# Two interleaved attention and gated-MLP layers on one core: operands, places and buffers in layer one's first gate/up pass

## The chip, the cores and the metric

The kernel runs on one core of one Trainium2 chip. The metric is device time in microseconds (us) of one execution; lower is better. The engines of a core are named as the profile names them: PE (TensorE matmul), PEld (its weight load), DVE (VectorE), ACT (ScalarE), POOL (GpSimd) and SP (SyncE, which in this kernel issues every transfer). SBUF is the on-chip working memory, PSUM the accumulation memory of 8 banks that PE writes.

## The reference

The same two blocks are applied twice, with a layer norm ahead of each and a residual sum behind each:

```python
def _B_ref(x, w_gate, w_up, w_down):
    g = jnp.einsum("bsd,df->bsf", x, w_gate)
    u = jnp.einsum("bsd,df->bsf", x, w_up)
    h = g * u
    return jnp.einsum("bsf,fd->bsd", h, w_down)
...
x = A_x
x = x + _A_ref(_layernorm(x, axis=-1), A_wqkv, A_wo)
x = x + _B_ref(_layernorm(x, axis=-1), B_w_gate, B_w_up, B_w_down)
x = x + _A_ref(_layernorm(x, axis=-1), A_wqkv, A_wo)
x = x + _B_ref(_layernorm(x, axis=-1), B_w_gate, B_w_up, B_w_down)
```

`_A_ref` is linear attention with 32 heads. There are 2048 tokens of width 1024, the hidden width of the MLP is 3584, and all inputs are bf16.

## The kernel before

**What is in SBUF.** Everything lies in one arena with fixed byte offsets. `x_res` (offset `O_X`) holds the residual stream as 16 rows of 128 tokens by 1024. `xnT` holds the normalised tokens, transposed. Every operation is recorded with the byte ranges that it reads and writes (pages of 32 bytes), and a planner makes the semaphore waits from these ranges alone. So an operation waits for an earlier one where their recorded ranges meet, also where the data that it uses does not. The order of each engine's instructions is the order in which the Python code records them.

**Layers.** A layer is attention (`layer_A`) and then the MLP (`layer_B`). The MLP works in two passes of 1024 tokens (rows 0 to 7, rows 8 to 15). A pass is `gateup` (gate and up projections, and their product, the hidden values `hA` to `hD`) and then `down`. At the end of attention the output projection (L1494) runs token row by token row, with DVE and ACT evicting its banks, and the work that readies the first gate/up pass is fed in between.

**Products.** Each large matmul is done by a scheme of Strassen's kind: both factors are cut into two by two blocks, and seven products of block sums stand for eight of blocks. In a gate/up pass the token factor is `xnT` cut by half of the width and by half of the 1024 tokens. Its four sums T1, T2, T4 and one made in place come from `t_ops`. The weight factor is 256 columns of the gate weights or of the up weights, cut by half of the width (`h`) and by half of the columns (`c`). Its four sums come from `prep_s` (L916), and are written to `w_scratch` in DRAM, where later passes find them. 256 hidden columns, gate and up, make a **pair**; there are 14 pairs, 0 to 13, and in the words below A is the gate half of a pair, B the up half.

**Second level.** In layer one's first pass products 1 and 5 of pairs 1 to 13 are cut once more: the token block of product 1 (`xblk(0, s0)`) and that of product 5 (T1) are cut by `tp_ops` (L886) into quarters, and four sums are made of them. Three of the sums have buffers of their own; the third in order is written **in place** over one quarter (b12). The matching weight sums are made pair by pair by `sums0` (L1748), in rows 3 to 6 of `x_res`: pair 1 uses rows 5 and 6, pair 2 rows 3 and 4, and so on in turn. Pair 0 stays at one level and reads the whole blocks. The sub-products (`l2_of`, L1635) record the whole block as read whichever quarter they use:

```python
b11, b12, b21, b22 = [(x[:, 2 * k:2 * k + 2, 256 * c:256 * c + 256], rx) for k in range(2) for c in range(2)]
```

**The order of a pair.** `emit` (L1794) records tokens of a hand-written list, once for each pair; a quote mark means the pair before, a plus the pair behind:

```python
(False, 0): "S1+ D2A M3B' P5A T1 P1B R0 P7A 57 P6B S5+ M5A D4A M2A 11+ P7B D3A 16+ D2B M4A P5B M3A R1 T0+ M2B M5B 51+ D4B P1A+ 56+ 17+ D3B P6A+ M4B",
```

P is a product (P1B is product 1 of the up half), D one of the products 2, 3, 4 that close a bank, M an eviction to the hidden values, and S1 and S5 the weight sums of the second level. 11, 16 and 17 are the sub-products of product 1 that both halves share (11 stands for two), 51, 56 and 57 those of product 5. T stores the weight sums of one pair or makes those of a later one, and also carries steps that prepare the down weights (`wd_load`, `wd_prep`). R issues the next weight load into a ring of five slots. One-level products are recorded at L1584 (four matmuls of 512 columns each), sub-products at L1654 (two matmuls of 256 columns each).

**Buffers of this pass.** `x_res` is lent out while the pass runs. At its start `stash` writes rows 3 to 7 to DRAM (`x_scratch`), and `tail` (L1846) loads them back when `down` begins. Row 7 is `O_MB`: in `mul0` (L1759) ACT evicts the gate half into its first half and the up half into its second, and DVE adds a partial product to both and multiplies them. The partial products of P6 (`cpb(0, c)`) and P7 (`cpb(1, c)`) lie at `O_CP`, one buffer each, for every pair. `mul0` uses them for hidden blocks "3" (P6's) and "2" (P7's).

**DVE, SP and the down pass.** The functions `tt` (L839) and `stt` (L842) record nearly all DVE work, so these two lines stand for many things. SP issues transfers in the order of the program and waits at each for the ranges that it needs. At the start of `down` SP issues the five row loads and then the loads of `b_load`, which bring down weights to DVE for their second-level sums. The evictions of `down` add each bank to a row of `x_res` or to a temporary.

Of the kernel before, what the change touches and what calls it, by code (L numbers as in the profile page):

```python
# [180 lines left out]
def build_kernel(nc, A_x, A_wqkv, A_wo, B_w_gate, B_w_up, B_w_down, out):  # L181
    _, S, D = A_x.shape
# [90 lines left out]
            "1": [RB + 28672 + i * 1024 for i in range(3)], "5": [O_SX[4], RC + NR * SZ_SLOT, O_X1]}  # L273
    O_TP0 = dict(O_TP, **{"5": [RE + 6144, RC + NR * SZ_SLOT, O_X1]})
    O_C50 = {"1": RE + 4096, "5": RE + 5120}
    O_MB = O_X + 7 * D * 2
    O_DOUT = [O_R + 8192, RE]
    O_CP = O_R + 12288
    O_SS = {"3": O_R + 4096, "2": O_R + 6144}
# [54 lines left out]
    with ExitStack() as es:  # L334
# [13 lines left out]
        def vh(o, n):  # L348
            return ah[:, o // 2: o // 2 + n]
# [367 lines left out]

        RG = {}
        XQ = []

        def ring_begin(first):
            RG.update(n=0, first=first, tq=False)
# [163 lines left out]
        def tp_ops(pair, prods, jit):  # L886
            s0 = pair * 1024
            res = []
            for q in prods:
                if q == "5":  # L890
                    x, base, st_ = T1, O_T, 1024
                else:
                    kb, s1 = (0 if q == "1" else 1), s0 + (512 if q == "3" else 0)
                    x, base, st_ = xblk(kb, s1), O_XT + 4 * kb * S * 2 + s1 * 2, S * 2
                ot = (O_TP0 if jit else O_TP)[q]
                tp = [vh(o, 512).rearrange("p (k s) -> p k s", s=256) for o in ot]
                rt = [R(o, 1024) for o in ot]
                b11, b12, b21, b22 = [x[:, 2 * k:2 * k + 2, 256 * c:256 * c + 256] for k in range(2) for c in range(2)]
                r11, r12, r21, r22 = [_seg(base + 2 * k * st_, 2, st_, c * 512, (c + 1) * 512) for k in range(2) for c in range(2)]
                res += [(lambda tp=tp, rt=rt, a=b12, b=b11, ra=r12, rb=r11: tt(tp[0], a, b, ALU.subtract, ra + rb, rt[0])),  # L900
                        (lambda tp=tp, rt=rt, a=b22, ra=r22: tt(tp[1], a, tp[0], ALU.subtract, ra + rt[0], rt[1])),
                        (lambda a=b22, b=b12, ra=r22, rb=r12: tt(b, a, b, ALU.subtract, ra + rb, rb)),
                        (lambda tp=tp, rt=rt, a=b21, ra=r21: tt(tp[2], a, tp[1], ALU.subtract, ra + rt[1], rt[2]))]
            return res

        def wt(o):
# [9 lines left out]
        def prep_s(n):  # L916
            a, b = sorted([(n + 1) % NR, (n + 2) % NR])
            ring = [f(O_SLOT, NR * SZ_SLOT // 2).rearrange("p (s x) -> p s x", s=NR)[:, a:b + 1:b - a] for f in (vb, vh)]

            def w(h, c):  # L920
                return ring[0][:, :, 1024 * h:1024 * h + 1024].rearrange("p s (k c) -> p s k c", c=256)[:, :, :, 128 * c:128 * c + 128]

            def rg(lo, hi):
                return r_slot(n, lo, hi) + r_slot(n + 1, lo, hi)
            sv = [ring[1][:, :, 2048 + 512 * i:2560 + 512 * i].rearrange("p s (k c) -> p s k c", c=128) for i in range(4)]
            a11, a12, a21, a22 = w(0, 0), w(0, 1), w(1, 0), w(1, 1)
            ra = rg(0, 4096)
# [624 lines left out]
        def layer_B(lnp, nxt, first):  # L1552
            is_last = nxt is None

            def pair(ps_, p, l2):
# [5 lines left out]
                for ab_ in range(2):  # L1561
# [5 lines left out]
                    else:  # L1567
# [7 lines left out]
                xb = {"1": (xblk(0, s0), r_xblk(0, s0)), "2": (xblk(1, s0), r_xblk(1, s0)), "3": (xblk(1, s0 + 512), r_xblk(1, s0 + 512)),  # L1575
                      "4": (T4, rT[2]), "5": (T1, rT[0]), "6": (T2, rT[1]), "7": (xblk(0, s0 + 512), r_xblk(0, s0 + 512))}

                def cpb(i, c):
                    o = O_CP + (2 * i + c) * 1024
                    return vh(o, 512), R(o, 1024)  # L1580

                def pe(q, c, bank, start):
# [176 lines left out]
                def mul0(c, dst, bank, i):  # L1759
                    ho = H[dst][1]  # L1760
                    j = units[c]["j"]
                    hx, hr = H[dst][0][:, j, :], R(ho + j * 1024, 1024)
                    mb, rb = vh(O_MB, 1024), R(O_MB, 2048)
                    P.add("act", lambda e: e.activation(mb[:, 512 * c:512 * c + 512], psb(bank), AF.Copy, scale=SG), prd=[bank],
                          wr=R(O_MB + 1024 * c, 1024))
                    if c:
                        o = O_CP + 2 * i * 1024
                        tt(mb, mb, vh(o, 1024), ALU.add, rb + R(o, 2048), rb)
                        tt(hx, mb[:, 0:512], mb[:, 512:1024], ALU.mult, rb, hr)

# [15 lines left out]
            def gateup(ps_, ticks, l2):  # L1786
# [7 lines left out]
                def emit(it, tk):  # L1794
# [16 lines left out]
                            x_pop()  # L1811
                    if tk[0] == "P":
                        c["p" + tk[1]](x)
                    elif tk[0] == "D":
                        c["fin"](tk[1], x)
                    elif tk[0] == "M":
# [29 lines left out]
                def tail():  # L1846
# [447 lines left out]
            def run():  # L2294
# [91 lines left out]
```

## Time and profile before

| what | value |
|---|---|
| median of 3 runs | 1435.49 us (1435.11 to 1437.32) |
| the profiled execution's span | 1433.4 us |
| median less span | 2.1 us (launch and end, which lie outside the span) |
| layer one's first gate/up pass on PE | about 231.7 to 402.2 us of the span, shared with the last output projections until 237.7 |
| layer one's first down pass on PE | from 402.2 us |
| one pair in the steady part of the pass | 11.7 us (its groups of PE start at 257.64 and again at 269.50, 281.18) |

The profile is of one execution on the core. It has no device time of its own beside its span. A row of the timeline gives the start, the length, the engine and line, the operation, the number of instructions merged, and in square brackets the idle time of the engine just before and what ended it. A matmul's length in it is from its start to the modelled end of its flow through the array; the next one starts before that, so the spacing of matmuls is shorter than their length.

### The profile page before, as it was taken

To read this page: it belongs to the slowest core of one execution; us is meant where nothing else is said; L and a number is where in the kernel's file an instruction comes from. 1 tells how busy PE (TensorE), PEld (TensorE's weight loads), DVE (VectorE), ACT (ScalarE), POOL (GpSimd) and SP (SyncE) were. 2 spreads that over 40 slices of the span, in tenths; PEclk is the share of its full clock that TensorE was granted. 3 is DMA by queue.
4 is the path that set the end of the run, shared out by engine and by line. 5 is a ranking of instruction groups with operands and counts; after the bars stand their busy time and mean duration, and the time that the engine had idled before them with its cause. 6 is when DMAs were issued, how large, how long until landed. Compare 5 with 4: busy or idle time off the path is not lost.

```text
span 1433.4 us, 22057 instructions
## 1 busy us (share of the span) xinstructions
PE 1422.9 (99%) x8248; PEld 801.1 (56%) x8304; DVE 1140.8 (80%) x2048; ACT 700.2 (49%) x1478; POOL 225.6 (16%) x265
## 2 busy tenths in 40 slices
PE   9999999999999999999999999999999999999999
PEld 4444444555544555554664444456666477666548
DVE  7878887888867799877678878779877787777856
ACT  4752367766710255550156523667776016777401
POOL 4643632000000000000034345300000000000000
PEclk9999999999999999999999999999999999999999
DMA  7416867987889899986898067689976699777657
GB/s 235 108 26 188 180 136 192 285 290 256 291 282 343 258 270 290 273 274 234 247 358 225 28 175 166 131 236 275 283 244 205 223 300 314 260 261 257 205 163 241
DMA packets 386091, 330.00 MB, mean 230 GB/s; under 512 B 178368, under 2 KB 333888, under 8 KB 385472
## 3 DMA queue, kind: packets, MB, share of 16 engines
q1 hardware_dynamic: 385984, 328.59, 76.8%
q8 instruction: 65, 1.06, 0.3%
q14 instruction: 42, 0.34, 0.1%
HBM read 240.71 MB, written 64.23 MB: 213 GB/s over the span
## 4 chain that ended last, share of the span: by engine, by line
PE 96%; DVE 2%; ACT 1%; issue 1%; DMA 0%; POOL 0%; SPq 0%; ACTq 0%
PE ps L1584 27%; PE ps L1654 18%; PE ps L2154 16%; PE ps L1494 8%; PE ps L1396 8%; PE ps L1162 6%; PE ps L2049 6%; PE ps L966 5%; PE ps L976 3%; DVE arena L839 1%; PE ps L1408 1%; PE ps L1436 0%; DVE arena L842 0%; ACT arena L492 0%; DMA arena<-in_B_w_gate_dram 0%
## 5 line engine op out<-in xcount | busy, mean ns | idle before, releaser
L839 DVE TENSOR_TENSOR arena<-arena 128x512 f16<-128x512 f16 (+9 forms) x776 | 429.2, 579 | 74.3 <-ACT arena L1698 45.1
L1584 PE MATMUL ps<-arena 128*128 128x512 f16 x1808 | 446.8, 379 | 0.6 <-ACT ps L1614 0.6
L842 DVE SCALAR_TENSOR_TENSOR arena<-ps,arena 128x512 f16<-128x512 f32 (+2 forms) x440 | 293.2, 684 | 75.4 <-PE ps L2154 52.2
L1654 PE MATMUL ps<-arena 128*128 128x256 f16 x2324 | 312.1, 273 | 0.8 <-ACT arena L1698 0.6
L1654 PEld LDWEIGHTS ps<-arena 128*128 128x128 f16 (+1 forms) x2324 | 226.3, 98 | 104.1 <-DVE ps L1673 3.5
L1584 PEld LDWEIGHTS ps<-arena 128*128 128x128 f16 (+1 forms) x1808 | 176.5, 98 | 141.7 <-ACT ps L1614 1.1
L2154 PE MATMUL ps<-arena 128*128 128x512 f16 (+1 forms) x1053 | 229.9, 379 | 0.6
L1589 ACT ACTIVATE arena<-ps 128x512 f16<-128x512 f32 x224 | 134.0, 598 | 92.9 <-PE ps L1584 90.6
L2154 PEld LDWEIGHTS ps<-arena 128*128 128x128 f16 x1064 | 104.1, 98 | 124.7
L1670 ACT COPY ps<-ps 128x256 f32<-128x256 f32 x220 | 81.1, 369 | 127.5 <-PE ps L1654 121.3
L1673 DVE TENSOR_TENSOR ps<-ps,arena 128x256 f32<-128x256 f32 x220 | 92.1, 427 | 37.2 <-PE ps L1654 19.9
L1396 PE MATMUL ps<-arena 128*128 128x512 bf16 x499 | 114.1, 379 | 0.7
L2053 ACT COPY ps<-ps 128x256 f32<-128x256 f32 x36 | 12.9, 357 | 204.9 <-PE ps L2049 204.9
L1494 PE MATMUL ps<-arena 128*128 128x512 bf16 x500 | 110.7, 379 | 0.6
L483 POOL TENSOR_SCALAR arena<-arena 128x1 f32<-128x1 f32 x43 | 16.3, 380 | 589.9 <-DVE arena L482 589.9
L2049 PE MATMUL ps<-arena 128*128 128x256 f16 (+1 forms) x882 | 97.8, 273 | 0.1
L1162 PE MATMUL ps<-arena 128*128 128x512 bf16 (+1 forms) x412 | 94.7, 379 | 0.8 <-DVE ps L1166 0.3
L2049 PEld LDWEIGHTS ps<-arena 128*128 128x128 f16 x882 | 85.7, 98 | 11.9 <-DVE arena L842 0.7
L1302 POOL TENSOR_TENSOR arena<-arena 128x1024 f16<-128x1024 f32 x32 | 79.1, 2473 | 70.3 <-DVE arena L1300 61.6
L1614 ACT COPY ps<-ps 128x512 f32<-128x512 f32 x112 | 64.2, 573 | 50.0 <-PE ps L1654 45.2
L1001 POOL TENSOR_TENSOR arena<-arena 128x512 f32<-128x512 f32 x60 | 73.5, 1244 | 69.4 <-DVE arena L1091 33.7
L1494 PEld LDWEIGHTS ps<-arena 128*128 128x128 f16 x512 | 50.1, 98 | 59.8
(78 smaller groups left out, 1223.3 us busy)
## 6 DMA issues: line engine op xcount, KB each, us to landing
arena<-w_scratch SPq DMA_DIRECT2D x84, 512.0 KB, 5.1
arena<-sp_scratch SPq DMA_DIRECT2D x56, 512.0 KB, 5.9
arena<-t_scratch SPq DMA_DIRECT2D x29, 896.0 KB, 6.6
arena<-in_B_w_down_dram SPq DMA_DIRECT2D x20, 896.0 KB, 7.3
w_scratch<-arena SPq DMA_DIRECT2D x28, 512.0 KB, 6.2
sp_scratch<-arena SPq DMA_DIRECT2D x28, 512.0 KB, 4.1
arena<-in_B_w_gate_dram SPq DMA_DIRECT2D x42, 256.0 KB, 5.1
arena<-in_B_w_up_dram SPq DMA_DIRECT2D x42, 256.0 KB, 3.7
```

The lines of the kernel that those rows point to most:

```text
L839: P.add("dve", lambda e: e.tensor_tensor(out=out, in0=a, in1=b, op=op), rd=rd, wr=wr, prd=prd)
L842: P.add("dve", lambda e: e.scalar_tensor_tensor(out=out, in0=a, scalar=sc, in1=b, op0=ALU.mult, op1=op1), rd=rd, wr=wr, prd=prd)
L1162: P.add("pe", lambda e: [e.matmul(psb(bank), x[:, k, :], w[:, k, :], start=(start and k == 0), stop=(k == 3), skip_group_check=True) for k ...
L1396: return [e.matmul(psb(bank), xr[:, t, j * 128:(j + 1) * 128], pk[:, h, t, :], start=(t == 0), stop=(t == NST - 1)) for t in range(NST)]
L1494: return [e.matmul(psb(bank), xnT[:, g, i * 128:(i + 1) * 128], wp[:, g, dh * 512:(dh + 1) * 512], start=(dh == 0 and g == 0), stop=(g == ...
L1584: P.add("pe", lambda e: [e.matmul(psb(bank), w[:, k, :], x[:, k, :], start=(start and k == 0), stop=(k == 3), skip_group_check=True) for k ...
L1589: P.add("act", lambda e: e.activation(t, psb(bank), AF.Copy, scale=SG), prd=[bank], wr=r)
L1654: P.add("pe", lambda e: [e.matmul(psb(bank)[:, 256 * half:256 * half + 256], w[:, k, :], xx[:, k, :], start=(start and k == 0), stop=(k == ...
L1670: P.add("act", lambda e: e.copy(psb(dst[c])[:, 0:256], lo), prd=[bk], pwr=[dst[c]])
L1673: P.add("dve", lambda e: e.tensor_tensor(out=psb(dst[c])[:, 256:512], in0=lo, in1=c5, op=ALU.add), prd=[bk], rd=rc5, pwr=[dst[c]])
L2049: P.add("pe", lambda e: [e.matmul(psb(bank)[:, 256 * half:256 * half + 256], a[:, k, :], w[:, k, :], start=(start and k == 0), stop=(k == ...
L2154: return [e.matmul(psb(bank), hv[:, 7 * hf + k, t * 128:(t + 1) * 128], w[:, k, :], start=(start and hf == 0 and k == 0), stop=(hf == 1 an ...
```

## The change

The scheme of products stays; operands, places and buffers of the one pass change.

- In `prep_s` the names a12 and a21 change places, so a12 is now the second half of the width with the first half of the columns. The count, the shapes and the recorded ranges of the four operations are as before.
- In this pass the third of the four operations of `tp_ops`, the in-place one, is no longer in the list that the end of attention works off. It is kept in `XD`, and `emit` records it directly behind P1B (for product 1) and P5B (for product 5) of pair 0, the last readers of the whole blocks.
- The partial products of P6 get a second buffer in row 1 of `x_res` (`O_X + D * 2`), for odd pairs.
- `O_MB` becomes two buffers: row 7 for hidden block "2" and row 2 for "3".
- So rows 1 and 2 are lent out as well: `stash` stores seven rows, 1 to 7, and `tail` of this pass loads seven rows back. Other passes keep five.

```diff
-    O_MB = O_X + 7 * D * 2
+    O_MB = {'2': O_X + 7 * D * 2, '3': O_X + 2 * D * 2}
...
-                res += [(lambda tp=tp, rt=rt, a=b12, b=b11, ra=r12, rb=r11: tt(tp[0], a, b, ALU.subtract, ra + rb, rt[0])),
...
+                ops = [(lambda tp=tp, rt=rt, a=b12, b=b11, ra=r12, rb=r11: tt(tp[0], a, b, ALU.subtract, ra + rb, rt[0])),
+                       (lambda tp=tp, rt=rt, a=b22, ra=r22: tt(tp[1], a, tp[0], ALU.subtract, ra + rt[0], rt[1])),
+                       (lambda a=b22, b=b12, ra=r22, rb=r12: tt(b, a, b, ALU.subtract, ra + rb, rb)),
+                       (lambda tp=tp, rt=rt, a=b21, ra=r21: tt(tp[2], a, tp[1], ALU.subtract, ra + rt[1], rt[2]))]
+                if jit:
+                    XD[q] = ops.pop(2)
+                res += ops
...
-            a11, a12, a21, a22 = w(0, 0), w(0, 1), w(1, 0), w(1, 1)
+            a11, a12, a21, a22 = w(0, 0), w(1, 0), w(0, 1), w(1, 1)
...
+                def o_cp(i):
+                    return O_X + D * 2 if first and ps_ == 0 and p % 2 and not i else O_CP + 2048 * i
+
                 def cpb(i, c):
-                    o = O_CP + (2 * i + c) * 1024
+                    o = o_cp(i) + c * 1024
...
-                    mb, rb = vh(O_MB, 1024), R(O_MB, 2048)
+                    mb, rb = vh(O_MB[dst], 1024), R(O_MB[dst], 2048)
...
-                        o = O_CP + 2 * i * 1024
+                        o = o_cp(i)
...
                         c["p" + tk[1]](x)
+                        if jit and p == 0 and tk in ("P1B", "P5B"):
+                            XD[tk[1]]()
...
-                    for t in range(5):
-                        i = 8 * ps_ + 3 + t
+                    for t in range(1 if jit else 3, 8):
+                        i = 8 * ps_ + t
...
-                for k in range(5):
-                    stash(3 + k)
+                for k in range(1 if first else 3, 8):
+                    stash(k)
```

On PE, ACT and POOL the instructions stand in the same order as before, and only their waits differ. Because the code grew, the lines of the changed kernel are higher: L839, L1584, L1654, L1673 of before are L840, L1591, L1661, L1680 there.

**DVE at the start of the pass**, from the norm of the last token row that is readied here (L506) to the first step on the down weights (128x1024). The rows 128x256 are the second-level weight sums S5 of pair 1, the row with `ps` is the bank join of sub-product 16, and 128x2x256 is the in-place operation. Before:

```order
L506 TENSOR_SCALAR arena<-arena 128x1024 [waits d_tl0,s_pool]
L839 TENSOR_TENSOR arena<-arena 128x256
L839 TENSOR_TENSOR arena<-arena 128x256 [waits s_dve]
L839 TENSOR_TENSOR arena<-arena 128x256
L839 TENSOR_TENSOR arena<-arena 128x256 [waits s_dve]
L1673 TENSOR_TENSOR ps<-ps,arena 128x256 [waits s_pe]
L839 TENSOR_TENSOR arena<-arena 128x1024 [waits d_dr]
```

and in the changed kernel:

```order
L506 TENSOR_SCALAR arena<-arena 128x1024 [waits d_tl0,s_pool]
L840 TENSOR_TENSOR arena<-arena 128x2x256 [waits s_pe]
L840 TENSOR_TENSOR arena<-arena 128x256
L840 TENSOR_TENSOR arena<-arena 128x256 [waits s_dve]
L840 TENSOR_TENSOR arena<-arena 128x256
L840 TENSOR_TENSOR arena<-arena 128x256 [waits s_dve]
L1680 TENSOR_TENSOR ps<-ps,arena 128x256 [waits s_pe]
L840 TENSOR_TENSOR arena<-arena 128x2x256 [waits s_pe]
L840 TENSOR_TENSOR arena<-arena 128x1024 [waits d_dr]
```

The two in-place operations have come down from the end of attention to these two places, each with a wait for PE: the first for P1B, the second for P5B.

**PE at the same place**, from P6B to 51. Before (x4 of L1584 is one product, x2 of L1654 one sub-product; D2B and P5B are the row with x8):

```order
L1584 MATMUL ps<-arena 128x512 [waits s_act]
L1584 MATMUL ps<-arena 128x512 x3
L1654 MATMUL ps<-arena 128x256 [waits d_rr3]
L1654 MATMUL ps<-arena 128x256
L1654 MATMUL ps<-arena 128x256 [waits s_dve]
L1654 MATMUL ps<-arena 128x256
...
L1654 MATMUL ps<-arena 128x256 [waits s_dve,s_act]
L1654 MATMUL ps<-arena 128x256
L1584 MATMUL ps<-arena 128x512 x8
L1654 MATMUL ps<-arena 128x256 [waits s_dve]
L1654 MATMUL ps<-arena 128x256
```

and in the changed kernel:

```order
L1591 MATMUL ps<-arena 128x512 [waits s_act]
L1591 MATMUL ps<-arena 128x512 x3
L1661 MATMUL ps<-arena 128x256 [waits s_dve]
L1661 MATMUL ps<-arena 128x256 x3
...
L1661 MATMUL ps<-arena 128x256 [waits s_act]
L1661 MATMUL ps<-arena 128x256
L1591 MATMUL ps<-arena 128x512 x8
L1661 MATMUL ps<-arena 128x256 [waits s_dve]
L1661 MATMUL ps<-arena 128x256 x3
```

The first two rows of L1661 are 11 of pair 1, the last two are 51. Each now waits on DVE once, at its first matmul, and since a sub-product records the whole block as read, what it waits for is the in-place operation on that block.

**SP at the start of the pass.** Before, and then in the changed kernel:

```order
L591 DMA_TRANSPOSE arena<-arena 128x8x128 [waits s_dve] x2
L440 DMA x_scratch<-arena 128x1024 x5
L440 DMA arena<-in_B_w_down_dram 128x4x1024
L440 DMA w_scratch<-arena 128x2048 x2
L591 DMA_TRANSPOSE arena<-arena 128x8x128 [waits s_dve]
```

```order
L591 DMA_TRANSPOSE arena<-arena 128x8x128 [waits s_dve] x2
L440 DMA x_scratch<-arena 128x1024 x7
L440 DMA arena<-in_B_w_down_dram 128x4x1024
L440 DMA w_scratch<-arena 128x2048 x2
L591 DMA_TRANSPOSE arena<-arena 128x8x128 [waits s_dve]
```

The stores go out in the order of the rows, so rows 5 and 6 are the third and fourth store before and the fifth and sixth now. At the start of `down` the loads back become x7 in the same way, and the first two of them wait for DVE.

More of the change, by code (lines that the diff above doesn't have):

```diff
@@ L719, in build_kernel @@
         XQ = []
+        XD = {}
         def ring_begin(first):
@@ L899, in tp_ops @@
                 r11, r12, r21, r22 = [_seg(base + 2 * k * st_, 2, st_, c * 512, (c + 1) * 512) for k in range(2) for c in range(2)]
-                res += [(lambda tp=tp, rt=rt, a=b12, b=b11, ra=r12, rb=r11: tt(tp[0], a, b, ALU.subtract, ra + rb, rt[0])),
-                        (lambda tp=tp, rt=rt, a=b22, ra=r22: tt(tp[1], a, tp[0], ALU.subtract, ra + rt[0], rt[1])),
-                        (lambda a=b22, b=b12, ra=r22, rb=r12: tt(b, a, b, ALU.subtract, ra + rb, rb)),
-                        (lambda tp=tp, rt=rt, a=b21, ra=r21: tt(tp[2], a, tp[1], ALU.subtract, ra + rt[1], rt[2]))]
+                ops = [(lambda tp=tp, rt=rt, a=b12, b=b11, ra=r12, rb=r11: tt(tp[0], a, b, ALU.subtract, ra + rb, rt[0])),
[5 more added lines that the diff above has]
+                res += ops
             return res
@@ L1762, in mul0 @@
                     hx, hr = H[dst][0][:, j, :], R(ho + j * 1024, 1024)
-                    mb, rb = vh(O_MB, 1024), R(O_MB, 2048)
+                    mb, rb = vh(O_MB[dst], 1024), R(O_MB[dst], 2048)
                     P.add("act", lambda e: e.activation(mb[:, 512 * c:512 * c + 512], psb(bank), AF.Copy, scale=SG), prd=[bank],
-                          wr=R(O_MB + 1024 * c, 1024))
+                          wr=R(O_MB[dst] + 1024 * c, 1024))
                     if c:
-                        o = O_CP + 2 * i * 1024
+                        o = o_cp(i)
                         tt(mb, mb, vh(o, 1024), ALU.add, rb + R(o, 2048), rb)
```

## The prediction

> **What bounds the kernel.** First the head of the page, and the shares of the chain of waits.
>
> ```profile
> span 1433.4 us, 22057 instructions
> PE 1422.9 (99%) x8248; PEld 801.1 (56%) x8304; DVE 1140.8 (80%) x2048; ACT 700.2 (49%) x1478; POOL 225.6 (16%) x265
> ...
> PE 96%; DVE 2%; ACT 1%; issue 1%; DMA 0%; POOL 0%; SPq 0%; ACTq 0%
> ```
>
> PE is busy for all but 1433.4 - 1422.9 = 10.5 us, so a change that leaves its instructions alone can gain little, and costs just what it adds to PE's idle time. The windows and the waits of the changed pass say how much idle time there is in it (columns of a window: length, then busy us of PE, PEld, DVE, ACT, POOL, granted clock, DMA share, GB/s; of a wait: total us, times, longest).
>
> ```profile
> 240.00:250.00 10.00, 9.40 (x49) 4.42 (x47) 7.97 (x19) 8.12 (x18) 2.10 (x4) 1.00 1.04 296
> 250.00:262.00 12.00, 12.00 (x72) 6.84 (x70) 9.23 (x23) 9.10 (x21) 0.55 (x2) 1.00 0.77 245
> ...
> PE ps L1584 <- ACT ps L1614: 0.6, 1, 0.6
> ```
>
> One stall of 0.6 us near 243, and no other in the pass. That is all that loosened waits could give back there. The question is then which waits the change puts in front of PE, and I read the timelines of PE, DVE and SP around the start of the pass.
>
> ```profile
> 242.96 1.90 PE L1584 MATMUL ps<-arena 128*128 128x512 f16 x8 [0.58 <-ACT ps L1614]
> 244.70 0.60 PE L1654 MATMUL ps<-arena 128*128 128x256 f16 x4
> ...
> 246.86 0.38 PE L1654 MATMUL ps<-arena 128*128 128x256 f16 x2
> 247.08 1.89 PE L1584 MATMUL ps<-arena 128*128 128x512 f16 x8
> 248.81 0.60 PE L1654 MATMUL ps<-arena 128*128 128x256 f16 x4
> ...
> 253.57 0.82 PE L1654 MATMUL ps<-arena 128*128 128x256 f16 x6
> ```
>
> By the order of the tokens these are P6B and D4A (242.96), 11 of pair 1 (244.70), 16 (246.86), D2B and P5B (247.08), 51 (248.81), and P5A and P1B of pair 1 (253.57). P1B of pair 0 is two products ahead of 242.96.
>
> ```profile
> 240.59 0.55 DVE L506 TENSOR_SCALAR arena<-arena 128x1024 f16<-128x1024 bf16 x1 [3.71 <-POOL arena L496]
> 241.05 3.55 DVE L839 TENSOR_TENSOR arena<-arena 128x256 f16<-128x256 bf16 x8
> 244.51 0.54 DVE L506 TENSOR_SCALAR arena<-arena 128x1024 f16<-128x1024 bf16 x1
> 244.97 1.01 DVE L839 TENSOR_TENSOR arena<-arena 128x256 f16<-128x256 f16 x4
> 247.28 0.43 DVE L1673 TENSOR_TENSOR ps<-ps,arena 128x256 f32<-128x256 f32 x1 [1.30 <-PE ps L1654]
> 247.63 2.61 DVE L839 TENSOR_TENSOR arena<-arena 128x1024 f16<-128x1024 bf16 x4
> ...
> 251.81 0.75 DVE L1673 TENSOR_TENSOR ps<-ps,arena 128x256 f32<-128x256 f32 x2
> ...
> L839 DVE TENSOR_TENSOR arena<-arena 128x512 f16<-128x512 f16 x4 | 1.6, 420 | 0.0
> ```
>
> The x8 at 241.05 are S1 of pair 1 (four) and `prep_s` (four), the x4 at 244.97 are S5, 247.28 is the join of 16, 247.63 `wd_prep`. The last line is the group that holds the in-place operations, at the end of attention: 512 elements, 420 ns each.
>
> **The change, part by part.**
>
> *The in-place operation of product 1* now stands behind the L506 of 244.51. P1B is long done there, so DVE does not wait; it starts in S5's slot at 244.97, takes 0.42, and ends at 245.39. Sub-products 11 read the same recorded block, so PE must wait for that end, where it used to start at 244.70. A handoff costs 0.04 to 0.05 us (16 ends at 247.24 and DVE starts at 247.28). PE starts at 245.44: a stall of **0.74 us**. S5 behind it moves by about 0.4, inside the 1.30 us that DVE then idled.
>
> *The in-place operation of product 5* waits for P5B and 51 waits for it, and 51 is the very next thing on PE. P5B ends at 247.08 + 1.89 = 248.97; plus 0.04, 0.42 and 0.05 makes 249.48, against a start at 248.81: **0.67 us**, wherever the whole sequence then lies. This is a full round trip, and only the last 0.16 of P5B's flow was hidden before.
> Behind it on DVE are `wd_prep`, the eviction M2B, two steps of M5B, and the joins of 56 and 17. Before, `wd_prep` started 1.18 us ahead of 51 (247.63 against 248.81), now about 0.13 ahead; so the joins come 1.05 late in PE's time, and end at 251.81 + 0.43 + 1.05 = 253.29 (0.43 is the join at 247.28) and 251.81 + 0.75 + 1.05 = 253.61. P5A asks for the first at 253.57, and P1B, four sub-product matmuls (0.43 us) later at 254.00, for the second. Both hold, by 0.3 and 0.4 us: nothing. If that cover were gone, each us of DVE costs one of PE.
>
> *Two more stores.* The two loaned rows are stored first, so rows 5 and 6, into which S1 of pair 1 writes, leave two places later. Here are SP's rows and the landing times (minimum, median, maximum) of the first two stores, of the last two, and of the load for `wd_prep`.
>
> ```profile
> 236.54 2.73 SPq L440 DMA_DIRECT2D x_scratch<-arena  x5
> 239.31 0.62 SPq L440 DMA_DIRECT2D arena<-in_B_w_down_dram  x1
> ...
> DMA to landing us min/median/max: 2.3/2.4/2.4
> ...
> DMA to landing us min/median/max: 2.8/3.1/3.5
> ...
> DMA to landing us min/median/max: 7.2/7.2/7.2
> ```
>
> The stores are issued some 0.5 apart, and land 2.3, 2.4, then up to 2.8 and 3.5 us after their issue. Today the third and fourth land at about 240.2 and 240.9, just before S1 asks for them (241.05 for row 5, two operations of 0.25 later, 241.55, for row 6). Now row 5's is the fifth, issued near 238.6, and row 6's the sixth, near 239.2. At 2.4 us each they land at 241.0 and 241.6: no delay. At the last store's 3.5 and a rise as steep behind it (some 4.0) row 6 lands at 243.2: S1's third operation is 1.7 late. The last store of today competed with the 1 MB load that follows it, which now comes two stores later, so I take a point between: 242.5, **1.0 us** late (0 to 1.7). S1, `prep_s`, L506 and the in-place operation are one unbroken stretch of DVE, so the delay reaches 11 in full.
> `wd_prep` needs its load: 239.31 + 7.2 = 246.5 before; two more issues (1.1) and 0.5 MB at 296 GB/s (1.8) make 249.4. DVE comes to it at 249.4 plus the first stall of 1.7, or 251.1: covered.
>
> *Weight blocks, second partial-product buffer, second eviction buffer:* the same operations with the same shapes, and fewer waits on ACT. The one such wait seen is in the drain of the pass, where M3B waits for DVE while PE runs on:
>
> ```profile
> 402.24 34.05 PE L2154 MATMUL ps<-arena 128*128 128x512 bf16 x155
> ...
> 402.37 0.60 ACT L1764 ACTIVATE arena<-ps 128x512 f16<-128x512 f32 x1 [1.28 <-DVE arena L839]
> ```
>
> Nothing on PE comes of it. The end of attention loses two DVE operations and others move up; DVE idles there for POOL (the 3.71 above), so nothing too.
>
> *Two more loads at `down`.* DVE's rows, then SP's, then the landing of the row loads and of `b_load`:
>
> ```profile
> 408.26 0.69 DVE L842 SCALAR_TENSOR_TENSOR arena<-ps,arena 128x512 f32<-128x512 f32 x1 [1.33 <-PE ps L2154]
> ...
> 416.76 0.96 DVE L839 TENSOR_TENSOR arena<-arena 128x1536 f16<-128x1536 f16 x1 [3.79 <-DMA arena<-t_scratch]
> 419.05 0.29 DVE L839 TENSOR_TENSOR arena<-arena 128x256 f16<-128x256 f16 x1 [1.32 <-DMA arena<-t_scratch]
> ...
> 421.93 0.68 DVE L842 SCALAR_TENSOR_TENSOR arena<-ps,arena 128x512 bf16<-128x512 f32 x1
> ...
> 406.52 3.17 SPq L440 DMA_DIRECT2D arena<-x_scratch  x5
> 409.74 16.97 SPq L440 DMA_DIRECT2D arena<-t_scratch  x8
> ...
> DMA to landing us min/median/max: 5.2/5.5/5.7
> ...
> DMA to landing us min/median/max: 7.0/8.0/8.4
> ```
>
> The eviction at 408.26 now needs row 1, which lands at 406.52 + 5.2 = 411.7: 3.5 us late. DVE idled 3.79 and 1.32 us behind it for `b_load`, and that absorbs it. But `b_load` stands behind two more loads: 2 x 3.17 / 5 = 1.3 us of issue, or with another 0.5 MB at the 296 GB/s above up to 3.1 in all. DVE is then 1.3 to 3.1 late at 421.93, the eviction that frees the first bank of the second product (end 422.61). PE takes this bank again for the third product, eight groups of 14 matmuls after 402.24; at a spacing of (1.90 - 0.38) / 7 = 0.217 that is 426.5. The margin is 3.9 us: nothing.
>
> **The sum:** 0.74 + 1.0 + 0.67 = 2.4 us onto the profiled span, 1435.8. The median of the runs shown lies 2.1 above that span; 1435.8 + 2.1 = **1437.9 us**, or 0.17% slower. With the bounds of the stores (0 and 1.7) 1436.9 to 1438.6. Below about 0.2%, 2.9 us or 1438.4, a measurement of this kernel cannot tell it from no change. So: no change that can be told, leaning to the slow side.
>
> **Rivals.**
>
> *The stores are the larger part* (27%). From 1.5 us of delay on S1 the sum passes 2.9, and the change is slower. For it: landing times rise along the row, and the DMA share was 1.04 in that window. Against: five stores alone reached no more than 3.5. At 1.7 to 2.2 it gives 3.1 to 3.6: 1438.6 to 1439.1, slower.
>
> *The loads at `down` stall PE* (8%). If `b_load` comes 5 to 6 us later, 1.1 to 2.1 us of stall follow: 1439.0 to 1440.0, slower. Against it, 3.1 was the most that issue and bytes gave.
>
> *PE cools* (5%). Granted clock is 1.00 in the windows, the 0.6 stall included, but the first matmuls of the program run long:
>
> ```profile
> 1.36 4.45 PE L447 MATMUL ps<-arena 128*128 128x512 f16 x10 [1.36 <-POOL arena L443]
> 7.38 1.04 PE L976 MATMUL ps<-arena 128*128 128x512 bf16 x4 [0.46 <-ACT arena L599]
> ```
>
> Ten took 4.45 us, where a spacing of 0.217 and a flow of 0.38 make 2.3; at 7.38 the pace is full. If two stalls 4 us apart brought that back once, it costs 2.1 more: 1440.0, slower. The Trainium skill, "TensorE: Matmul & The Clock Gate", section "The HAM clock gate (the "warmup" mystery)", has the array fall to half its clock after an idle window of about 3.4 us. By that rule stalls of 1.7 and 0.7 are too short and this rival gives nothing; the 0.6 stall without a slower matmul behind it agrees, and no row of this pass shows a longer one.
>
> *The stalls are shorter or hidden* (7%). If something else on the way to 11 were late already, only the round trip stays: 1435.5 + 0.7 = 1436.2, no change. Against it: PE's row at 244.70 shows no wait.
>
> *The change gains* (3%): the 0.6 stall goes and the second round trip costs nothing, 1434.9; that is still within 0.2%, and what could pass it is only a drift of the measurement itself.
>
> **How the numbers follow.** The forecast as worked out has 50%, and with the shorter stalls (7%) within 0.2% has 57%. The stores, the loads and the clock make 27 + 8 + 5 = 40% slower; faster 3%. The range must reach both signs: from 1435.3, a little under the case of shorter stalls, to 1440.0, where the last two rivals end; the likeliest case's own is 1436.9 to 1438.6.
>
> **What would show it.** In the changed profile, around 245 us, PE's sub-products of 11 should carry an idle time of 1.3 to 2.5 us put down to DVE, and 51 one of 0.6 to 0.7, with a 128x512 group of DVE between P5B and 51. S1 should start late or wait for `x_scratch`. The rest of the pass should keep its rhythm from pair to pair, and all later starts should be shifted by one and the same amount. DVE should idle near 409 to 414 for `x_scratch`, without a wait on PE. Wrong would be: a stall of PE that comes back in each pair, one in the first `down`, or 11 starting without a wait.

## The result and the profile after

| | median us | runs |
|---|---|---|
| before | 1435.66 (1434.96 to 1437.32) | 11 |
| changed | 1438.91 (1437.34 to 1441.06) | 11 |

The ratio is 1.0022, with a 95% interval of 1.0013 to 1.0031: 3.25 us slower. That is a change clear of noise, just past the 2.9 us below which the prediction would have called it none, and 1.0 us above the forecast of 1437.9. The profiled execution of the changed kernel took 1439.2 us, with a span of 1437.5. One execution among the experiments, the profiled one of e7_all, took 5025 us where the other ten took 1435.1 to 1436.6, so its profile is left out (its time is one of the 11 in the median) and the same kernel was run again as e7b_all.

The head of the page, and the chain of waits:

```profile
span 1437.5 us, 22075 instructions
PE 1422.7 (99%) x8248; PEld 801.1 (56%) x8304; DVE 1141.0 (79%) x2048; ACT 700.3 (49%) x1478; POOL 226.0 (16%) x265
...
PE 92%; DVE 3%; DMA 2%; ACT 1%; issue 1%; SPq 1%; POOL 0%; DVEq 0%
```

PE's busy time is that of before to 0.2 us, so the whole loss is idle time of PE. DVE, DMA and SP, which held 2% of the chain together, now hold 6%. Where that idle time lies is in the waits of PE (total us, times, longest):

```profile
PE ps L1661 <- DVE arena L840: 1.6, 2, 1.1
PE ps L1661 <- DVE ps L1680: 1.4, 1, 1.4
...
PE ps L970 <- DMA arena<-in_A_wqkv_dram: 0.9, 1, 0.9
...
PE ps L1591 <- ACT ps L1621: 0.6, 1, 0.6
```

and on its timeline:

```profile
242.84 1.90 PE L1591 MATMUL ps<-arena 128*128 128x512 f16 x8 [0.58 <-ACT ps L1621]
245.81 0.61 PE L1661 MATMUL ps<-arena 128*128 128x256 f16 x4 [1.06 <-DVE arena L840]
...
250.61 0.61 PE L1661 MATMUL ps<-arena 128*128 128x256 f16 x4 [0.52 <-DVE arena L840]
...
280.52 0.83 PE L1661 MATMUL ps<-arena 128*128 128x256 f16 x6 [1.42 <-DVE ps L1680]
```

The 0.58 us is that of before. Then come 11 of pair 1 and 51, as forecast, and a third stall that was not: P5A of pair 2, which waits for DVE's join. The idle time is counted from the modelled end of the matmul before. An unstalled matmul starts 0.38 - 0.22 = 0.16 us ahead of that end, so a stall costs PE its idle time plus 0.16: **1.22, 0.68 and 1.58 us**, 3.48 in all. Measured from P6B (242.96 and 242.84), the down pass started at 159.28 us before (402.24) and starts at 162.80 now (405.64): 3.52 later, the same sum. The 0.9 us at the weights of layer two lies outside the pass and changes from one execution to the next: it is 0.2 in a second profile of this kernel, 0.9 again in e7b_all, where the three stalls are gone, and not among the waits of the one profile before. Whether the change makes it more frequent is open.

DVE at the same place:

```profile
241.22 3.74 DVE L840 TENSOR_TENSOR arena<-arena 128x256 f16<-128x256 bf16 x8 [0.20 <-DMA x_scratch<-arena]
244.88 0.54 DVE L506 TENSOR_SCALAR arena<-arena 128x1024 f16<-128x1024 bf16 x1
245.33 1.35 DVE L840 TENSOR_TENSOR arena<-arena 128x512 f16<-128x512 f16 x5
...
250.13 2.96 DVE L840 TENSOR_TENSOR arena<-arena 128x512 f16<-128x512 f16 x5 [1.29 <-PE ps L1591]
...
275.84 2.62 DVE L840 TENSOR_TENSOR arena<-arena 128x1024 f16<-128x1024 bf16 x4 [2.11 <-DMA arena<-in_B_w_down_dram]
```

S1 waits for its stores: it starts 0.75 us after the start of the L506 ahead of it (0.46 before), 0.20 of that idle, and takes 0.19 longer (3.74 against 3.55). That makes 0.48 us. The two in-place sums head the groups at 245.33 and 250.13; ahead of the second DVE stands still for 1.29 us until P5B ends. The last row is `wd_prep` of the second step on the down weights: it waits 2.11 us for its load, where it waited 0.46 before. Here are SP's rows that lead to that load, before

```profile
257.73 0.98 SPq L440 DMA_DIRECT2D w_scratch<-arena  x2
258.76 2.90 SPq L591 DMA_TRANSPOSE arena<-arena  x1
261.70 2.91 SPq L440 DMA_DIRECT2D t_scratch<-arena  x4
264.65 0.57 SPq L440 DMA_DIRECT2D arena<-in_B_w_down_dram  x1
...
DMA to landing us min/median/max: 7.7/7.7/7.7
```

and in the changed kernel:

```profile
260.56 0.82 SPq L440 DMA_DIRECT2D w_scratch<-arena  x2
261.42 2.25 SPq L591 DMA_TRANSPOSE arena<-arena  x1
263.71 3.54 SPq L440 DMA_DIRECT2D t_scratch<-arena  x4
267.29 0.66 SPq L440 DMA_DIRECT2D arena<-in_B_w_down_dram  x1
...
DMA to landing us min/median/max: 8.5/8.5/8.5
```

The first row is a store of weight sums that DVE makes, so it goes out when DVE has made them; all behind it on SP follows at once. Counted from P6B, this store is issued 2.95 us later than before, of which PE's own two stalls are 1.90; the other 1.05 is DVE's lateness against PE. SP then took 0.19 less for the rows between, so the load is issued at 24.45 us from P6B against 21.69 before, 0.86 later in PE's time. On top it landed 0.8 us slower.

### The profile page after: what moved, and what is told of

Its sections match the earlier page's. It is cut to its first block, busy times and chain, and to the rows that moved or that the text cites. A ratio compares the mean times of both kernels' runs of the same rounds, so it can differ in the third digit from the quotient of the medians.

```text
span 1437.5 us, 22075 instructions
## 1 busy us (share of the span) xinstructions
PE 1422.7 (99%) x8248; PEld 801.1 (56%) x8304; DVE 1141.0 (79%) x2048; ACT 700.3 (49%) x1478; POOL 226.0 (16%) x265
## 3 DMA queue, kind: packets, MB, share of 16 engines
q8 instruction: 65, 1.06, 0.3%
## 4 chain that ended last, share of the span: by engine, by line
PE 92%; DVE 3%; DMA 2%; ACT 1%; issue 1%; SPq 1%; POOL 0%; DVEq 0%
PE ps L1591 25%; PE ps L1661 17%; PE ps L2163 16%; PE ps L1400 8%; PE ps L1498 6%; PE ps L1166 6%; PE ps L2058 6%; PE ps L970 5%; PE ps L980 3%; DVE arena L840 2%; DMA arena<-in_A_wqkv_dram 1%; DMA arena<-in_B_w_down_dram 1%; SPq L440 1%; PE ps L1412 0%; PE ps L1440 0%
## 5 line engine op out<-in xcount | busy, mean ns | idle before, releaser
L840 DVE TENSOR_TENSOR arena<-arena 128x512 f16<-128x512 f16 (+9 forms) x776 | 429.9, 581 | 77.0 <-ACT arena L1705 45.1
L1591 PE MATMUL ps<-arena 128*128 128x512 f16 x1808 | 446.8, 379 | 0.6 <-ACT ps L1621 0.6
L1661 PE MATMUL ps<-arena 128*128 128x256 f16 x2324 | 312.1, 273 | 3.7 <-DVE arena L840 1.6
L1661 PEld LDWEIGHTS ps<-arena 128*128 128x128 f16 (+1 forms) x2324 | 226.2, 98 | 107.6 <-DVE ps L1680 5.2
L1591 PEld LDWEIGHTS ps<-arena 128*128 128x128 f16 (+1 forms) x1808 | 176.6, 98 | 141.6 <-ACT ps L1621 1.1
L1680 DVE TENSOR_TENSOR ps<-ps,arena 128x256 f32<-128x256 f32 x220 | 92.3, 428 | 36.5 <-PE ps L1661 19.4
```

The lines of the kernel that those rows point to most:

```text
L840: P.add("dve", lambda e: e.tensor_tensor(out=out, in0=a, in1=b, op=op), rd=rd, wr=wr, prd=prd)
L1591: P.add("pe", lambda e: [e.matmul(psb(bank), w[:, k, :], x[:, k, :], start=(start and k == 0), stop=(k == 3), skip_group_check=True) for k ...
L1661: P.add("pe", lambda e: [e.matmul(psb(bank)[:, 256 * half:256 * half + 256], w[:, k, :], xx[:, k, :], start=(start and k == 0), stop=(k == ...
L1680: P.add("dve", lambda e: e.tensor_tensor(out=psb(dst[c])[:, 256:512], in0=lo, in1=c5, op=ALU.add), prd=[bk], rd=rc5, pwr=[dst[c]])
```

## The experiments

All go back to the same question: which part makes which stall. "Chain" is the theory formed from the two profiles: the moved in-place sums make all three stalls, the third by way of DVE, SP and the second load. The rivals stand in each expectation. Medians are of 11 runs; the kernel before took 1435.88, 1436.20 and 1435.95 us in the three groups (e1 to e4; e5, e6, e7_all and e9; the last three).

| kernel | median us | ratio to before, 95% | PE's loss at 11, 51, P5A of pair 2 in its profile, us |
|---|---|---|---|
| e1_in_list | 1435.78 | 0.9999 (0.999 to 1.0008) | 0, 0, under 0.3 |
| e2_five_rows | 1438.22 | 1.0016 (1.0007 to 1.0025) | 0.74, 0.68, under 0.3 |
| e3_load_first | 1437.14 | 1.001 (1.0001 to 1.0018) | 1.21, 0.68, 0 |
| e4_quarters | 1436.44 | 1.0005 (0.9996 to 1.0013) | 0, 0, under 0.2; 0.45 at P5A of pair 1 |
| e5_only_1 | 1437.53 | 1.001 (1.0001 to 1.0019) | 1.21, 0, 0.62 |
| e6_only_5 | 1437.84 | 1.0009 (1.0 to 1.0018) | 0, 0.68, 1.77 |
| e7_all | 1436.01 | 0.9996 (0.9987 to 1.0005) | not read |
| e9_stash_last | 1438.37 | 1.0015 (1.0006 to 1.0023) | 0.74, 0.68, 0.60 |
| e7b_all | 1435.43 | 0.9992 (0.9983 to 1.0001) | 0, 0, 0 |
| e8_load_behind | 1435.41 | 0.9998 (0.9989 to 1.0006) | 0, 0, 0 |
| after_again | 1438.54 | 1.0015 (1.0006 to 1.0024) | 1.19, 0.68, under 0.2 |

The losses are the idle times of the rows below plus 0.16. An entry "under" has no idle row, and is bounded by the time from P6B to P5A of pair 2, less 34.16 us (277.12 - 242.96, before) and less the stalls ahead of it. An interval is about 1.3 us to either side, so medians that lie closer than that do not rank the kernels, and the profiles size the stalls. A profile is of one execution, which can lie off the median by 1.7 us (e7b_all, 1437.15), so the losses do not add up to the medians.

**e1_in_list.** Both in-place sums go back.

```diff
-                if jit:
-                    XD[q] = ops.pop(2)
...
-                        if jit and p == 0 and tk in ("P1B", "P5B"):
-                            XD[tk[1]]()
```

> The changed kernel with both in-place sums back in the list that the end of attention works off; seven stores, seven loads and the new buffers stay. Pair 0 then reads two quarters that are already overwritten. Theory (chain): the loss is three stalls of PE, 1.2 us at 11, 0.7 at 51, 1.6 at P5A of pair 2, and all three come from the two moved operations, the third by way of DVE, SP and the second load for the down weights. Then none of the three is left here, and the time is that of before, 1435.7 (up to 1436.0). Rival (traffic): the third stall comes from the two extra stores; then it stays, and the time is about 1437.3.

Measured 1435.78, and the whole pass has one idle row on PE, that of before:

```profile
244.45 1.90 PE L1589 MATMUL ps<-arena 128*128 128x512 f16 x8 [0.58 <-ACT ps L1619]
```

Seven stores, seven loads, the second buffers and the weight blocks together cost nothing that can be told. The loss needs the two moved operations; the traffic rival falls. e1 is a probe and no repair: as in the kernel before, where the last of these sums ends by 236.3 us and pair 0's products run on from 237.71, pair 0 reads quarters that the sums have already written over. The order that the change adds is what e1 leaves out.

**e2_five_rows.** The buffers and row numbers of before, with the moved sums.

```diff
-    O_MB = {'2': O_X + 7 * D * 2, '3': O_X + 2 * D * 2}
+    O_MB = {'2': O_X + 7 * D * 2, '3': O_X + 7 * D * 2}
...
-                    return O_X + D * 2 if first and ps_ == 0 and p % 2 and not i else O_CP + 2048 * i
+                    return O_CP + 2048 * i
...
-                for k in range(1 if first else 3, 8):
+                for k in range(3, 8):
```

> The changed kernel with the one partial-product buffer and the one eviction buffer of before, so five stores and five loads; the moved in-place sums stay. Partial products are then overwritten before their readers. Chain: 11 stalls by 1.0 (the 0.2 of waiting for a store goes), 51 by 0.7, P5A of pair 2 by 1.3 to 1.6: 1438.6. Traffic: the third stall is gone, 1437.2.

```profile
245.83 0.61 PE L1661 MATMUL ps<-arena 128*128 128x256 f16 x4 [0.58 <-DVE arena L840]
250.63 0.61 PE L1661 MATMUL ps<-arena 128*128 128x256 f16 x4 [0.52 <-DVE arena L840]
```

Partial products are overwritten ahead of their readers here as in the kernel before. Without the wait for stores 11 loses 0.74 us, so the two extra stores cost 1.22 - 0.74 = 0.48 of the first stall. 51 is unchanged. The third stall is not in this profile, though the median stays 2.3 us up: its load landed 7.3 us after its issue, not 8.5. The expectation of a steady 1.3 to 1.6 there was wrong; what varies is the landing. So this run does not tell the chain from the traffic rival, which had no third stall either.

**e3_load_first.** The load for the down weights goes ahead of the four stores.

```diff
-                        if j:
-                            wd_store(j - 1)
                         if j < NJ // 2:
                             wd_load(j)
+                        if j:
+                            wd_store(j - 1)
```

> The changed kernel with one thing moved: SP issues each load for the down weights ahead of the four stores of the step before, not behind them. Chain: the second load goes out about 3 us earlier, the third stall is gone, those at 11 and 51 stay: 1437.3. Traffic: the load lands late by contention wherever it is issued; 0.5 to 1.6 of the third stall stays, 1438 to 1438.9.

PE stalls as expected at 11 (1.05 idle) and 51 (0.52). `wd_prep` no longer waits, and the join that P5A of pair 2 needs is ready 0.7 us ahead of it (278.26 + 0.43 against 279.38):

```profile
274.07 2.61 DVE L840 TENSOR_TENSOR arena<-arena 128x1024 f16<-128x1024 bf16 x4
...
278.26 0.76 DVE L1680 TENSOR_TENSOR ps<-ps,arena 128x256 f32<-128x256 f32 x2
...
279.38 0.82 PE L1661 MATMUL ps<-arena 128*128 128x256 f16 x6
```

The load was issued at 264.18 and landed 7.4 us later, at 271.58, 2.5 us ahead of `wd_prep`; at the slowest landing of any profile, 8.7, it would still have been in time. The median is 1.26 us above that of before, against 3.25 and 2.59 for the changed kernel. When the load is issued decides, not the traffic.

**e4_quarters.** The recorded ranges are cut to the quarter that is used; the work is the same.

```diff
-                    b11, b12, b21, b22 = [(x[:, 2 * k:2 * k + 2, 256 * c:256 * c + 256], rx) for k in range(2) for c in range(2)]
+                    xo, xs_ = (O_T, 1024) if q == "5" else (O_XT + s0 * 2, S * 2)
+
+                    def rq(k, c):
+                        return _seg(xo + 2 * k * xs_, 2, xs_, c * 512, (c + 1) * 512) if jit else rx
+                    b11, b12, b21, b22 = [(x[:, 2 * k:2 * k + 2, 256 * c:256 * c + 256], rq(k, c)) for k in range(2) for c in range(2)]
```

> The changed kernel with the sub-products of this pass recorded as reading their quarter alone, so that 11 and 51 need not wait for the in-place sums. Chain: no stall at 11 and 51, but DVE still stands still until P5B ends and is later against PE than in the changed kernel (1.7 us against 1.0), so joins and the second load come later: 0.4 us at P5A of pair 1 and 1.6 to 2.3 at P5A of pair 2: 1437.7 to 1438.4. Rival (the two recorded waits are all that matters): 1435.7 to 1436.0.

PE no longer stalls at 11 or 51, so the first two stalls come from the recorded range and not from the data. DVE still stands still for 1.29 us, and since PE does not wait with it, that shows at P5A of pair 1:

```profile
249.76 2.96 DVE L840 TENSOR_TENSOR arena<-arena 128x512 f16<-128x512 f16 x5 [1.29 <-PE ps L1591]
...
254.78 0.83 PE L1665 MATMUL ps<-arena 128*128 128x256 f16 x6 [0.29 <-DVE ps L1684]
```

The 0.45 us was expected at 0.4. The third stall was not there, against the expectation: this load landed after 7.2 us. The median, 1436.44, lies between the rival's 1436.0 and the chain's 1437.7, and its interval (1435.3 to 1437.8) decides for neither; the 0.45 us in the profile is against the rival.

**e5_only_1 and e6_only_5.** One of the two moved sums each.

```diff
-                if jit:
+                if jit and q != "5":
                     XD[q] = ops.pop(2)
...
-                        if jit and p == 0 and tk in ("P1B", "P5B"):
+                        if jit and p == 0 and tk == "P1B":
```

e6 has "1" and P5B in these places.

> The changed kernel with the in-place sum of product 5 back in the list; only that of product 1 is moved. Pair 0's product 5 then reads a quarter that is already overwritten. Chain: a stall of 1.1 to 1.2 us at 11, none at 51, and none at P5A of pair 2, since DVE no longer stands still behind P5B: 1437.0. Rival (any late DVE makes the third stall): 1438.5.

> The changed kernel with the in-place sum of product 1 back in the list; only that of product 5 is moved. Pair 0's product 1 then reads a quarter that is already overwritten. Chain: no stall at 11, 0.7 us at 51, and at P5A of pair 2 anything from 0 to 1.6 us by how late the second load for the down weights lands: 1436.6 to 1438.2. Rival (the third stall needs both operations): 1436.6 at most.

Of e5, then of e6:

```profile
245.93 0.61 PE L1661 MATMUL ps<-arena 128*128 128x256 f16 x4 [1.05 <-DVE arena L840]
278.99 0.83 PE L1661 MATMUL ps<-arena 128*128 128x256 f16 x6 [0.46 <-DVE ps L1680]
```

```profile
249.88 0.61 PE L1661 MATMUL ps<-arena 128*128 128x256 f16 x4 [0.52 <-DVE arena L840]
279.97 0.83 PE L1661 MATMUL ps<-arena 128*128 128x256 f16 x6 [1.61 <-DVE ps L1680]
```

Each sum makes its own one of the first two stalls. The third came in both, so the rival that it needs both operations falls: with a landing of 8.4 us e5 lost 0.62 there, where the chain had expected nothing, and with 8.7 e6 lost 1.77. In e5 the load was issued at 22.87 us from P6B, which less the stall of 1.21 is 21.66, no later against PE than before. So there the slow landing alone made the stall, and the kernel before, with 0.1 us to spare at 7.7, would pay about the same at such a landing (an estimate; no profile of it shows one). What the wait behind P5B adds is the 0.86 us of lateness.

**e9_stash_last.** Rows 3 to 7 are stored first, then 2 and 1.

```diff
-                for k in range(1 if first else 3, 8):
+                for k in (3, 4, 5, 6, 7, 2, 1)[:7 if first else 5]:
```

> The changed kernel with rows 3 to 7 stored first and rows 2 and 1 behind them. Chain: the stall at 11 falls from 1.2 to 1.0, 51 keeps 0.7, and the third stall is there or not as the second load lands 8.5 or 7.3 us after its issue: 1437.6 to 1439.0. Rival (the two extra stores ahead of rows 5 and 6 are what makes the changed kernel slow): 1436 to 1436.5.

```profile
245.61 0.61 PE L1661 MATMUL ps<-arena 128*128 128x256 f16 x4 [0.58 <-DVE arena L840]
250.41 0.61 PE L1661 MATMUL ps<-arena 128*128 128x256 f16 x4 [0.52 <-DVE arena L840]
...
279.33 0.83 PE L1661 MATMUL ps<-arena 128*128 128x256 f16 x6 [0.44 <-DVE ps L1680]
```

11 loses 0.74, as with five stores: the order of the stores was all that they cost. The rival that the stores are the main thing falls, at 1438.37. The third stall is 0.60 here although the load landed after 7.5 us, quicker than the 7.7 of before: its issue was 0.92 late in PE's time, so lateness alone makes a stall too.

**e7_all, e7b_all and e8_load_behind.** All repairs at once: those of e3, e4 and e9, and the in-place sum of product 5 behind sub-product 17 of pair 1. e8 is the same without that of e3.

```diff
-                        if jit and p == 0 and tk in ("P1B", "P5B"):
+                        if jit and p == 0 and tk == "P1B":
...
                         c["L"][tk[0]]["st" + tk[1]]()
+                        if jit and p == 1 and tk == "17":
+                            XD["5"]()
```

> The changed kernel with four things moved and no work left out: sub-products recorded by their quarter, the in-place sum of product 5 behind sub-product 17 of pair 1 where DVE does not wait for PE, rows 5 and 6 stored ahead of rows 1 and 2, each load for the down weights ahead of the four stores. Chain: none of the three stalls is left, and the time is that of before, 1435.5 to 1436.2. Rival (something else in the change costs about 1 us, such as the loads back at down or the start of layer two): 1436.7 to 1437.

> The kernel of e7_all once more, for a profile: quarters recorded, the in-place sum of product 5 behind sub-product 17, rows 5 and 6 stored first, each load for the down weights ahead of the four stores; no work left out. Chain: on PE only the 0.6 us stall that the kernel before has too; P5A of pair 2 starts with 0.5 us or more to spare; 1435.5 to 1436.2. Rival (the loads back at down or the start of layer two cost about 1 us): a wait of that size on PE there, 1436.7 to 1437.

> As e7b_all, but with the loads for the down weights behind the four stores again; no work left out. Chain: no stall at 11 and 51, DVE is 0.4 us later against PE than in the kernel before, and the second load lands 7.2 to 8.7 us after its issue, so P5A of pair 2 stalls by 0.2 to 1.6 us: 1436.0 to 1437.5. Rival (the order of load and stores does not matter once 11 and 51 are free): as e7b_all.

In e7b the pass has the 0.58 us of before and nothing else (what puts its profiled execution above its median lies outside: P6B starts at 244.34, 1.4 us later than before, and the 0.9 us at layer two), and P5A of pair 2 has 0.7 us to spare (277.38 + 0.43 against 278.50). The second pair of rows is e8's:

```profile
277.38 0.76 DVE L1684 TENSOR_TENSOR ps<-ps,arena 128x256 f32<-128x256 f32 x2
...
278.50 0.82 PE L1665 MATMUL ps<-arena 128*128 128x256 f16 x6
```

```profile
276.95 0.76 DVE L1684 TENSOR_TENSOR ps<-ps,arena 128x256 f32<-128x256 f32 x2
...
277.84 0.82 PE L1665 MATMUL ps<-arena 128*128 128x256 f16 x6
```

Both do all of the changed kernel's work in the time of the one before (1435.43 and 1435.41 against 1435.95), some 3 us under the changed kernel. In e8 the load left 0.54 us late in PE's time and landed after 6.8 us, the quickest of all, so that the stall expected of it did not come was luck in this profile; whether it comes in other executions its median does not show. Neither is shown to be faster than before: both intervals hold 1.

**after_again.** The changed kernel unchanged.

> The changed kernel unchanged, for a second profile. Chain: 1.2 us at 11 and 0.7 at 51 again to a tenth, while the third stall at P5A of pair 2 is the landing time of the second load plus 4.2 us of DVE work less PE's own time, so it may be anything from 0.2 to 1.8; about 1438.5. Rival (all three are fixed by the order of the program): the third is 1.6 us again.

```profile
245.82 0.61 PE L1661 MATMUL ps<-arena 128*128 128x256 f16 x4 [1.03 <-DVE arena L840]
250.62 0.61 PE L1661 MATMUL ps<-arena 128*128 128x256 f16 x4 [0.52 <-DVE arena L840]
...
279.09 0.83 PE L1661 MATMUL ps<-arena 128*128 128x256 f16 x6
...
DMA to landing us min/median/max: 7.2/7.2/7.2
```

The first two stalls come back to 0.03 us. The third is gone: the load was issued at 24.28 us from P6B, nearly as late as in the first profile (24.45), but landed after 7.2 us instead of 8.5. This splits the loss of the changed kernel into 1.9 us that are fixed by its order and a part that depends on one transfer.

**The third stall in all profiles.** Where the load stands behind the four stores, lateness of its issue and time of its landing together give the stall. Lateness is the time from P6B to the issue, less PE's stalls by then, less 21.69 us; the sum is lateness plus landing, less the 7.7 us and the 0.1 us to spare of before.

| profile | lateness, us | landing, us | sum, us | PE's loss at P5A of pair 2, us |
|---|---|---|---|---|
| changed, first | 0.86 | 8.5 | 1.56 | 1.58 |
| after_again | 0.72 | 7.2 | 0.12 | under 0.2 |
| e1 | 0.16 | 7.9 | 0.26 | under 0.3 |
| e2 | 0.74 | 7.3 | 0.24 | under 0.3 |
| e4 | 0.73 | 7.2 | 0.13 | under 0.2 |
| e5 | -0.03 | 8.4 | 0.57 | 0.62 |
| e6 | 0.88 | 8.7 | 1.78 | 1.77 |
| e9 | 0.92 | 7.5 | 0.62 | 0.60 |
| e8 | 0.54 | 6.8 | -0.46 | 0 |

The sum meets the loss to 0.05 us wherever a stall can be read, and the bounds elsewhere. Over the six profiles with 0.7 us of lateness or more the loss is 1.58, 1.77, 0.60 and three times little, some 0.7 on average, which with 1.9 makes 2.6; the medians of the changed kernel are 3.25 and 2.59 up. That this average is what the unprofiled runs see was not shown, nor how much of it the kernel before pays as well.

## Why the prediction came out as it did

The forecast was a loss of 2.4 us in a range of 1435.3 to 1440.0, leaning to the slow side; measured were 3.25 and, when the same kernel was timed again, 2.6. The side and the range were right and the waits at 11 and 51 were the right ones, but that the sum came so near is in part luck: in the first profile it had 0.5 us too much for the stores and lacked a third stall of 1.58. By its time alone, 1438.91 would fit the rival that the stores are the larger part (1438.6 to 1439.1), which the profile and e9 refute. Of the signs named, the idle time at 11 (1.3 to 2.5) was missed with 1.06, that at 51 (0.6 to 0.7) with 0.52, since the 0.16 us of hidden start is not in it, and later starts did not all shift by one amount, since P5A of pair 2 added its own.

- **What bounds the kernel:** right. PE's busy time did not move, and the whole loss is idle time in front of PE.
- **The in-place sum of product 1:** right where nothing else delays it, 0.74 us in e2 and e9.
- **The two more stores:** the mechanism was right, the size was not. The delay at 11 was taken as 1.0 of 0 to 1.7 and measured 0.48 (0.45 in the second profile). The step that failed is "a rise as steep behind it": the seven stores landed 2.4 to 3.5 us after their issue, no later than the five had.
- **The round trip at 51:** 0.67 forecast, 0.68 measured, in every kernel that has it.
- **The joins behind it in pair 1:** right. With the waits of PE they hold; e4 shows the 0.45 us that they cost when that cover goes.
- **"`wd_prep` needs its load ... covered":** right for the first load, the only one that was worked out. The failed step is that DVE's lateness of 1.05 us was taken as absorbed once the joins of pair 1 held. It went on through SP instead: DVE's weight sums, their store, issued just those 1.05 us late, everything queued behind that store, and with it the second load for the down weights. The third stall, 1.58 us in one profile and under 0.2 in the other, is what the sum lacked. The timeline of before had shown how little was to spare there: `wd_prep` waited 0.46 us for this load, and the join ended at 277.00, 0.1 us ahead of P5A:

```profile
276.57 0.76 DVE L1673 TENSOR_TENSOR ps<-ps,arena 128x256 f32<-128x256 f32 x2
...
277.12 0.82 PE L1654 MATMUL ps<-arena 128*128 128x256 f16 x6
```

- **The loads back at `down`:** right. The eviction waited for row 1 and came 3.66 us late in PE's time (415.32 - 408.26 - 3.40; 3.5 was forecast), `b_load` came 1.3 us later in PE's time (421.42 - 416.76 - 3.40), and PE did not wait (3.40 is how much later the down pass starts on PE, 405.64 - 402.24):

```profile
408.65 0.69 DVE L843 SCALAR_TENSOR_TENSOR arena<-ps,arena 128x512 f32<-128x512 f32 x1 [1.24 <-PE ps L2163]
415.32 0.69 DVE L843 SCALAR_TENSOR_TENSOR arena<-ps,arena 128x512 f32<-128x512 f32 x1 [4.98 <-DMA arena<-x_scratch]
...
421.42 0.96 DVE L840 TENSOR_TENSOR arena<-arena 128x1536 f16<-128x1536 f16 x1 [2.81 <-DMA arena<-t_scratch]
```

- **The rivals:** the stores turned out smaller than forecast, not larger. The loads at `down` and the clock stayed out; a stall of 1.42 us idle is followed by matmuls of the usual 0.27 us for 256 columns, with a granted clock of 1.00.

## What to carry to other kernels

When an operation is moved behind its readers, look at what is recorded as read: a range that is too wide turned one wait of DVE into a full round trip of PE, narrowing it took both round trips away (e4), and with the operation also placed where DVE does not wait for PE the move cost nothing that can be told (e7b_all, e8). Follow lateness on one engine through the stores that wait for it, since here every load queued behind such a store left late too; where a load has no time to spare, issue it ahead of stores that can wait. A margin that was 0.1 us in one profile is no margin when the transfer behind it varies by a microsecond or more.

## What was not expected of the hardware

The same 1 MB load at the same place of the program landed 6.8 to 8.7 us after its issue in the profiles of kernels that differ little (6.8 in e8, 7.2 in after_again, 7.7 before, 8.5 in the first profile of the changed kernel, 8.7 in e6). One and the same program had 8.5 in one execution and 7.2 in another, and with a difference of 0.17 us in the issue that made 1.4 us of PE's time (1.58 against under 0.2). Why the landing varies was not looked into.
